# A Mamba-2 scan and an expert merge on one core: another opening, and the carried state turned by half for odd sequences only

## The chip, the cores and the metric

The kernel runs on one core of a Trainium2 chip. The metric is the device time of one execution in microseconds (us). The engines are TensorE (PE, its weight loads PEld), VectorE (DVE), ScalarE (ACT), GpSimd (POOL) and SyncE (SP), which issues nearly all transfers (DMA) here; SP's and ACT's issues appear in the profile as SPq and ACTq. A page of the profile shows one execution. All arithmetic is in 32-bit floats; each matmul appears in the trace as two records, one for each of its two passes.

## What is computed

```python
# x (4, 8, 768, 32), a (4, 8, 768), B and C (4, 8, 768, 16), chunk = 32
for c in range(nc):
    cum = np.cumsum(la, axis=-1)                       # la = log of clipped a
    L = np.exp(cum[:, :, :, None] - cum[:, :, None, :]) * causal
    M = np.einsum('bhin,bhjn->bhij', Cc, Bc) * L
    y_intra = np.einsum('bhij,bhjd->bhid', M, xc)
    y_inter = np.einsum('bhin,bhnd->bhid', Cc, state) * np.exp(cum)[:, :, :, None]
    y[:, :, sl] = y_intra + y_inter
    Bx = np.einsum('bhjn,bhjd->bhjnd', Bc, xc) * decay_from_j[:, :, :, None, None]
    state = decay_full[:, :, None, None] * state + np.sum(Bx, axis=2)
# bridge: tokens (3072, 256); 4 experts, w1 (256, 1024), w2 (1024, 256)
p = domain_probs / (domain_probs.sum(-1, keepdims=True) + 1e-09)
for e in range(E):
    out += p[:, e:e + 1] * (np.maximum(x @ w1[e], 0.0) @ w2[e])
```

The kernel needs the same values and cuts them in its own way.

## The kernel before

The four sequences of 768 positions are cut into 12 steps of 64 positions; a step covers all four sequences and all eight heads. The heads lie as four quarters `q` of 32 partitions with two heads `t` in each. For a step `k`:

- `score` (L488) multiplies B with C: 32 small matmuls in eight tiles of the array. `ctm` is C with one of each pair of heads masked out (`mask`, L484).
- The decay matrix LT comes from a scan over rows of `a` (`scan`, L599); `masked` (L503) multiplies scores by LT into MT, `fade` (L507) puts the decayed B beside it.
- `carried` (L516) multiplies the state S with the decayed C: 16 matmuls, each 32x32, four for each quarter, one per sequence `s`. `inner` (L524) adds MT times x into the same four banks `ys[s]`.
- `keep_inner` (L537) copies the outputs into yT; `keep_state` (L540) copies the new state into A, and `carry` (L844) transposes A and adds the old state times its decay.

The tokens of yT go through the two layers of the experts (`product`, L875), with sums of weights and of tokens formed so that fewer products are needed; `gated` (L911) applies max and the gate, `snap` (L886) and `seed` (L891) copy between banks and SBUF. The gates of an expert are a row of `p_d` in DRAM, spread over all partitions by a transfer (`load_gate`, L863); the first expert's are spread by matmuls instead (`spread_gate`, L646).

**Order.** The opening (L551 to L711) is written out by hand, in program order for each engine: loads, constants, `spread` of the decays (L656), the turn of the gates (L639), the scores, scans, inner products and copies of step 0. Everything behind it is put in order by `Plan` (L84): PE's order is the list `line`; for the rest, the plan plays the kernel through with estimated durations, and chooses order, buffers ("homes") and, where two engines can do a thing, the engine. It starts PE at `START` and the other engines at offsets to it (L1426). `fetch` (L754) asks for a pair of steps' transfers: `bc` (B and C), `ab` (decays, broadcast from `acut_d`), `ct` (C turned to where its state lies), `dec` (decays broadcast from `dec_d`), `xb` (x).

**The turn.** For sequence s the result of `carried` for quarter q goes to quarter (q + s) mod 4. So `ct` is loaded rotated (seven transfers, L439), `dec` is read from an offset of `dec_d`, and `keep_state` copies back in pieces: 1, 4, 2 and 4 copies for the four sequences.

```python
rows, to = slice(32 * q, 32 * q + 32), 32 * ((q + s) % NQ)      # carried
n = (P, P // NQ, P // 2, P // NQ)[s]                            # keep_state
```

Of the kernel before, what the change touches and what calls it, by code (L numbers as in the profile page):

```python
# [23 lines left out]
START = 11.0  # L24
# [59 lines left out]
class Plan:  # L84
# [12 lines left out]
    def add(self, on, fn, reads=(), writes=(), part=(), lag=None, due=None, reuse=None, two=False,  # L97
            port=True, after=None, kb=0, hold=0.0, pieces=1, lead=None):
# [13 lines left out]
        for v in part:  # L112
            w.needs.update(v.readers)
            v.writers = v.writers + [w]
        w.needs.discard(w)
# [233 lines left out]
def kernel(  # L349
# [89 lines left out]
    def load_turned(m, ct):  # L439
        for s in range(NSEQ):  # L440
            src = xbc[s * NC + m][:, OCT:]
            lo = P // NQ * s
            nc.sync.dma_start(out=ct[:P - lo, s], in_=src[lo:])  # L443
            if lo:
                nc.sync.dma_start(out=ct[P - lo:, s], in_=src[:lo])
# [8 lines left out]
    def load_faded(m, dec):  # L454
        for s in range(NSEQ):
            src = dec_d[s, m, NT * s:NT * s + NH]
# [59 lines left out]
    def carried(ys, S, cts, first):  # L516
        for q in range(NQ):
            for s in range(NSEQ):
                rows, to = slice(32 * q, 32 * q + 32), 32 * ((q + s) % NQ)
# [17 lines left out]
    def keep_inner(s, yt, y):  # L537
        nc.scalar.copy(out=yt[:, :, s * L:s * L + L], in_=view(y)[:, :, 0:L])

    def keep_state(s, A, y, engine="ACT"):  # L540
        copy = nc.scalar.copy if engine == "ACT" else nc.vector.tensor_copy
        n = (P, P // NQ, P // 2, P // NQ)[s]
        for here in range(0, P, n):
            there = (here + P // NQ * s) % P
# [8 lines left out]
    a_dec = homes["V"][-2][:NSEQ * NC * NQ, 0]  # L553
# [5 lines left out]
    a_rows = a.rearrange("(p j k) (q t) s -> k j q p t s", p=NP, j=2, q=NQ)[0]  # L559
    for j, e in ((0, nc.sync), (1, nc.scalar)):  # L560
        e.dma_start(
            out=aq.rearrange("(q r) p t s -> r q p t s", q=NQ)[j], in_=a_rows[j])
    nc.scalar.dma_start(out=pr, in_=probs)
# [4 lines left out]
    load_forms(0, bc)  # L568
    load_tokens(0, xb)
    nc.sync.dma_start(out=a_sb, in_=a.rearrange("c (q t) s -> (c q) (t s)", t=NT))  # L570
# [28 lines left out]
    def scan(LT, src, lo):  # L599
# [7 lines left out]

    pairs = const.tile([P, T // P, 2], FP32)
# [11 lines left out]
    nc.gpsimd.tensor_copy(  # L620
        a_cut.rearrange("r (h t s) -> r h t s", h=2, t=NT),
        a_sb.rearrange("r (t h s) -> r h t s", h=2, t=NT))
    nc.gpsimd.memset(a_cut.rearrange("r (x s) -> r x s", s=L)[:, :, 0:1], 0.0)
    for s in range(NSEQ):
        n = NC * NQ
        nc.sync.dma_start(  # L626
            out=acut_d.rearrange("j k q h p t s -> p j (k q) h (t s)")[s // 2, s % 2],
            in_=a_cut[n * s:n * s + n].rearrange("r (h x) -> r h x", h=2))
    for fb in range(4, 8, 2):
        load_w1(fb, homes["W"][fb])  # L630
# [62 lines left out]
    for q in (2, 3):  # L693
        scan_quarter(0, LT, four[q], q)
# [780 lines left out]
```

## Time and profile before

| | us |
|---|---|
| median of 3 runs (lowest, highest) | 636.07 (635.37, 637.23) |
| the profiled execution | 636.93 |
| its span, first to last instruction | 635.1 |
| PE busy (matmuls) | 613.7 |
| VectorE busy | 504.8 |
| ScalarE busy | 289.9 |
| POOL busy | 145.5 |
| mean granted TensorE clock | 0.991 |

The DMA moved 123.72 MB, 195 GB/s on the mean. In the chain of work that ended last, PE has 88% of the span, DMA 6% and SP's queue 3%. Busy time of PE counts a matmul from its start to its modelled end, so neighbours overlap, and a matmul at a lower clock counts longer. A wait is put down to the instruction that released it. The times of a line are those of one execution.

### The profile page before, as it was taken

Reading aid. Unit: us, or ns where it says so; the run is one execution under the profiler, and the core shown is the slowest. Engines: PE = TensorE matmul, PEld = TensorE weight load, DVE = VectorE, ACT = ScalarE, POOL = GpSimd, SP = SyncE. Lnnn points to the kernel's source line nnn. Section 1 sums busy time; section 2 is a strip of 40 time slices with the busy share of each in tenths; the row PEclk is TensorE's granted clock in tenths of the full one; section 3 lists DMA queues with packets and bytes.
Section 4 is the critical chain, followed back from the end, with each engine's and each line's share of the span. In section 5 each row is a group of like instructions: output and inputs, shape, how many; then the busy total and the mean of one; then the engine's idle time right before and its main releaser. Section 6 shows DMA issues by size and latency. Waiting matters only on the chain.

```text
span 635.1 us, 11792 instructions
## 1 busy us (share of the span) xinstructions
PE 613.7 (97%) x4185; PEld 526.2 (83%) x4185; DVE 504.8 (79%) x887; ACT 289.9 (46%) x646; POOL 145.5 (23%) x163
## 2 busy tenths in 40 slices
PE   5988999999999999999999999999999999999995
PEld 2766788888888888888888888888888888888884
DVE  5279989899578588877878987969797977968783
ACT  2454465353345344644444344655443344555440
POOL 4021236534054247234545400000000000000000
PEclk9989989999999999999999999999999999999998
DMA  4597989879389878749999928546232329633002
GB/s 120 169 290 254 292 278 328 263 240 289 102 258 293 258 249 256 224 120 303 299 306 304 316 42 270 157 149 190 65 93 66 83 50 326 214 116 108 0 1 50
DMA packets 116418, 123.72 MB, mean 195 GB/s; under 512 B 29592, under 2 KB 84232, under 8 KB 116360
## 3 DMA queue, kind: packets, MB, share of 16 engines
q1 hardware_dynamic: 115988, 122.87, 62.8%
q8 instruction: 33, 0.54, 0.4%
q14 instruction: 25, 0.20, 0.1%
q10 hardware_dynamic: 372, 0.11, 0.1%
HBM read 97.94 MB, written 24.99 MB: 194 GB/s over the span
## 4 chain that ended last, share of the span: by engine, by line
PE 88%; DMA 6%; SPq 3%; DVE 1%; issue 1%; ACT 0%; POOL 0%; DVEq 0%; POOLq 0%; ACTq 0%
PE bank L879 85%; DMA bc<-in_xbc_dram 1%; DMA ab<-acut_d 1%; PE bank L531 1%; DMA w<-in_w_dram 1%; PE bank L494 1%; DMA v<-in_a_dram 1%; PE bank L520 1%; SPq L626 0%; SPq L443 0%; DMA ct<-in_xbc_dram 0%; DMA dec_d<-v 0%; SPq L465 0%; SPq L433 0%; SPq L457 0%
## 5 line engine op out<-in xcount | busy, mean ns | idle before, releaser
L879 PE MATMUL bank<-v,w 128*128 128x256 f32 x1816 | 433.0, 383 | 1.2 <-ACT gate L652 0.7
L879 PEld LDWEIGHTS bank<-v,w 128*128 128x128 f32 x1816 | 345.9, 192 | 52.5 <-issue 1.8
L879 PE MATMUL bank<-Y,w 128*128 128x256 f32 x824 | 211.9, 381 | 4.2 <-ACT bank L893 4.2
L906 DVE TENSOR_TENSOR v<-v,v 128x512 f32<-128x512 f32 x270 | 193.1, 746 | 25.7 <-ACT v L888 22.0
L879 PEld LDWEIGHTS bank<-Y,w 128*128 128x128 f32 x824 | 156.7, 191 | 27.0 <-ACT bank L893 5.5
L914 DVE SCALAR_TENSOR_TENSOR v<-bank,gate 128x512 f32<-128x512 f32 x172 | 117.2, 685 | 54.1 <-PE bank L879 38.9
L893 ACT COPY bank<-v 128x512 f32<-128x512 f32 (+1 forms) x201 | 111.9, 573 | 54.2 <-DVE v L906 34.4
L970 POOL TENSOR_TENSOR w<-w,w 128x256 f32<-128x256 f32 x97 | 94.5, 998 | 73.5 <-PE bank L879 36.3
L888 ACT COPY v<-bank 128x512 f32<-128x512 f32 x112 | 65.6, 585 | 97.4 <-PE bank L879 96.8
L1156 ACT COPY v<-bank 128x512 f32<-128x512 f32 x106 | 62.0, 585 | 99.3 <-PE bank L879 98.0
L906 POOL TENSOR_TENSOR v<-v,v 128x512 f32<-128x512 f32 x10 | 13.7, 1372 | 266.6 <-DVE v L906 164.5
L906 DVE TENSOR_TENSOR v<-bank,v 128x512 f32<-128x512 f32 x40 | 27.5, 688 | 10.0 <-PE bank L879 9.5
L1208 DVE TENSOR_TENSOR v<-v,v 128x256 f32<-128x256 f32 x54 | 22.0, 442 | 6.8 <-ACT v L1156 6.7
L601 DVE TENSOR_TENSOR_SCAN LT<-ab,diag 128x512 f32<-128x512 f32 x20 | 27.1, 1366 | 0.0
L1159 ACT COPY v<-bank 128x256 f32<-128x256 f32 x23 | 8.6, 373 | 38.1 <-PE bank L879 38.1
L970 POOL TENSOR_TENSOR w<-w 128x256 f32<-128x256 f32 x10 | 10.7, 1069 | 49.0 <-DVE v L906 24.8
L1055 DVE TENSOR_TENSOR bank<-bank,v 128x512 f32<-128x512 f32 x24 | 16.6, 692 | 5.9 <-PE bank L879 5.9
L797 POOL TENSOR_TENSOR u<-ct,dec 128x256 f32<-128x256 f32 x11 | 10.5, 957 | 41.9 <-DMA dec<-dec_d 18.3
L545 ACT COPY A<-bank 32x32 f32<-32x32 f32 (+2 forms) x61 | 10.8, 177 | 12.2 <-PE bank L531 11.6
L970 DVE TENSOR_TENSOR w<-w,w 128x256 f32<-128x256 f32 x41 | 16.2, 433 | 0.0
L531 PE MATMUL bank<-MT,xb 64*32 64x80 f32 (+1 forms) x768 | 11.7, 245 | 3.4 <-POOL MT L509 3.4
L505 DVE TENSOR_TENSOR MT<-bank,LT 128x512 f32<-128x512 f32 (+1 forms) x26 | 14.5, 618 | 0.4 <-PE bank L494 0.3
(77 smaller groups left out, 213.5 us busy)
## 6 DMA issues: line engine op xcount, KB each, us to landing
w<-w_d SPq DMA_DIRECT2D x138, 256.0 KB
w<-in_w_dram SPq DMA_DIRECT2D x126, 256.0 KB
w_d<-w SPq DMA_DIRECT2D x82, 256.0 KB
w<-in_w_dram SPq DMA_DIRECT2D x42, 128.0 KB
ab<-acut_d SPq DMA_DIRECT2D x20, 256.0 KB
xb<-in_xbc_dram SPq DMA_DIRECT2D x24, 192.0 KB
gate<-p_d SPq DMA_DIRECT2D x10, 384.0 KB
bc<-in_xbc_dram SPq DMA_DIRECT2D x6, 512.0 KB
```

Of the source, the lines that this page charges most:

```text
L505: engine.tensor_mul(MT[:, q, h, ..., 0:L], g, LT[:, q, h])
L531: nc.tensor.matmul(out=view(ys[2 * p + j])[32 * q:32 * q + 32, t, 0:w], lhsT=xb[rows, p, h * D:h * D + D], rhs=MT[rows, q, k % 2, p, t, 0: ...
L601: nc.vector.tensor_tensor_scan(out=LT.rearrange("r q h p t s -> r (q h p t s)")[:, lo:lo + w], data0=src, data1=diag.rearrange("r h s -> r ...
L879: nc.tensor.matmul(out=o, lhsT=w[:, j], rhs=x if half is None else x[:, j], start=(start and j == 0), stop=(j == 1), skip_group_check=True)
L888: act(.5, lambda e: nc.scalar.copy(out=flat(v), in_=bank.t), reads=[bank], writes=[v])
L893: act(.54 if to - lo > FB else .32, lambda e: nc.scalar.copy(out=bank.t[:, lo:to], in_=flat(v)[:, lo:to]), reads=[v], writes=[bank])
L906: plan.add(engines, lambda e: (on(e).tensor_add if sign > 0 else on(e).tensor_sub)(flat(v), whole(x), whole(y)), reads=[x, y], writes=[v], ...
L914: dve(D512, lambda e: nc.vector.scalar_tensor_tensor(out=h.t, in0=whole(x).rearrange("p (j m) -> p j m", j=JJ), scalar=0.0, in1=g.t[:, 2 * ...
L970: plan.add({"POOL": .72} if due else B256, lambda e, r=r, x=x, y=y, sign=sign: (on(e).tensor_add if sign > 0 else on(e).tensor_sub)(view(r ...
L1055: dve(D512, lambda e: nc.vector.tensor_sub(b5.t, b5.t, flat(t)), reads=[t], writes=[b5])
L1156: act(.5, lambda e: nc.scalar.copy(out=flat(v), in_=bank.t), reads=[bank], writes=[v])
L1208: plan.add(engines, lambda e: (on(e).tensor_add if sign > 0 else on(e).tensor_sub)(o[1](), x[1](), y[1]()), reads=[v for v in vs if v is n ...
```

## The change

In the opening:

- The probabilities `pr` are loaded first on ScalarE's queue, before the second half of `a`; the raw decays `a_sb` go before the tokens on SP's.
- Another idle matmul of two column blocks follows the first two, and three filler matmuls of 256 columns stand before `inner`.
- `turn_gates` and both `spread` come before `mask`; the stores of `p_d` go from ScalarE's queue to SP's.
- `spread_gate` comes right behind, before `score`, into the upper halves of two banks whose lower halves the scores use; two copies take the place of one.
- One quarter instead of two goes by way of ScalarE and POOL (`aside`); three instead of two are masked on VectorE.
- `a_dec` is one scan of 256 columns with restarts, instead of four scans; `dec_d` is stored before the copies of yT and A, which alternate ScalarE and VectorE for yT, and are on ScalarE for A.
- The cut decays (`a_cut`, the four stores into `acut_d`) and the first `ct` leave the opening for the planned part; the loads of `ab` get the stores as explicit needs. The weights w1 of blocks 4 and 6 and w2 of blocks 0 and 2 are loaded before `score` is written out.

In every step: the quarter for sequence s is (q + 2s) mod 4, so even sequences are not turned and odd ones by half. `ct` is loaded by three transfers instead of seven, `keep_state` needs 1, 2, 1 and 2 copies.

The plan's start goes from 11 to 10, and the engines' offsets are others.

```diff
-START = 11.0
+START = 10.0
...
     def load_turned(m, ct):
-        for s in range(NSEQ):
-            src = xbc[s * NC + m][:, OCT:]
-            lo = P // NQ * s
-            nc.sync.dma_start(out=ct[:P - lo, s], in_=src[lo:])
-            if lo:
-                nc.sync.dma_start(out=ct[P - lo:, s], in_=src[:lo])
+        src = xbc.rearrange("(p j k) r w -> k j r p w", p=NP, j=2)[m]
+        dst = ct.rearrange("r (p j) x -> j r p x", j=2)
+        nc.sync.dma_start(out=dst[0], in_=src[0][..., OCT:])
+        for h in range(2):
+            nc.sync.dma_start(
+                out=dst[1][L * h:L * h + L], in_=src[1][L - L * h:P - L * h][..., OCT:])
...
-            src = dec_d[s, m, NT * s:NT * s + NH]
+            src = dec_d[s, m, NH // 2 * (s % 2):][:NH]
...
-                rows, to = slice(32 * q, 32 * q + 32), 32 * ((q + s) % NQ)
+                rows, to = slice(32 * q, 32 * q + 32), 32 * ((q + 2 * s) % NQ)
...
-        n = (P, P // NQ, P // 2, P // NQ)[s]
+        n = P // (1 + s % 2)
         for here in range(0, P, n):
-            there = (here + P // NQ * s) % P
+            there = (here + L * (s % 2)) % P
...
+    nc.scalar.dma_start(out=pr, in_=probs)
     for j, e in ((0, nc.sync), (1, nc.scalar)):
         e.dma_start(
             out=aq.rearrange("(q r) p t s -> r q p t s", q=NQ)[j], in_=a_rows[j])
-    nc.scalar.dma_start(out=pr, in_=probs)
...
     load_forms(0, bc)
+    nc.sync.dma_start(out=a_sb, in_=a.rearrange("c (q t) s -> (c q) (t s)", t=NT))
     load_tokens(0, xb)
-    nc.sync.dma_start(out=a_sb, in_=a.rearrange("c (q t) s -> (c q) (t s)", t=NT))
...
-            nc.scalar.dma_start(
+            nc.sync.dma_start(
                 out=p_d.rearrange("e k h s x -> h (e k) s x")[h], in_=p_sb[:, L * h:L * h + L])
 
-    def spread_gate(bank, gate):
-        g = bank.rearrange("r (s x) -> r s x", s=NSEQ)
+    def spread_gate(banks, gate):
         for s in range(NSEQ):
             nc.tensor.matmul(
-                out=g[:, s], lhsT=ident[:rows, s:s + 1].to_broadcast([rows, P]),
-                rhs=p_sb, start=(s == 0), stop=True, skip_group_check=True)
-        nc.scalar.copy(
-            out=gate[:, :4].rearrange("r (h y) (z x) -> r h (y z) x", h=2, z=2),
-            in_=g.rearrange("r s (h x) -> r h s x", h=2))
+                out=banks[s // 2][:, P * (2 + s % 2):][:, :P],
+                lhsT=ident[:rows, s:s + 1].to_broadcast([rows, P]),
+                rhs=p_sb, start=(s % 2 == 0), stop=True, skip_group_check=True)
+        for p in range(NP):
+            nc.scalar.copy(
+                out=gate[:, :4].rearrange("r (h y) (z x) -> r h (y z) x", h=2, z=2)[:, :, 2 * p:2 * p + 2],
+                in_=banks[p][:, 2 * P:].rearrange("r (s h x) -> r h s x", s=2, h=2))
...
     idle(BANK[6])
     idle(BANK[7], 3)
+    idle(BANK[6], 2)
     spread(0, four)
-    mask(0, ctm, bc)
     turn_gates(seven[3])
     spread(1, four)
+    mask(0, ctm, bc)
+    spread_gate(seven[1:3], homes["gate"][0])
+    for fb in range(4, 8, 2):
+        load_w1(fb, homes["W"][fb])
+    for fb in range(0, 4, 2):
+        load_w2(fb, homes["W"][fb + 1])
     score([0], ctm, bc, seven)
-    for q in range(2):
+    for q in range(NQ):
         scan_quarter(0, LT, four[q], q)
-        aside(q, seven[q])
-    for q in (2, 3):
-        scan_quarter(0, LT, four[q], q)
+        if q == 0:
+            aside(q, seven[q])
     fade(0, MT, xb, LT)
-    for q in (2, 3):
+    for _ in range(3):
+        nc.tensor.matmul(
+            out=seven[0][:, 2 * P:], lhsT=one.to_broadcast([P, P]),
+            rhs=one.to_broadcast([P, 2 * P]), start=True, stop=True, skip_group_check=True)
+    for q in (1, 2, 3):
         masked(nc.vector, [0], q, MT, parts(seven[q], 1), LT)
     inner(0, seven, xb, MT, L + N, True)
-    for s in range(NSEQ):
-        keep_inner(s, yT0, seven[s])
-    keep_state(0, A0, seven[0])
-    spread_gate(seven[0], homes["gate"][0])
-    for s in range(1, NSEQ):
-        keep_state(s, A0, seven[s])
-    for i in range(4):
-        nc.vector.tensor_tensor_scan(
-            out=a_dec[:, L * i:L * i + L], data0=a_sb[:, L * i:L * i + L],
-            data1=zeros[:NSEQ * NC * NQ, :L], initial=1.0, op0=ALU.mult, op1=ALU.add)
+    nc.vector.tensor_tensor_scan(
+        out=a_dec, data0=a_sb, data1=a_first, initial=0.0, op0=ALU.mult, op1=ALU.add)
     for z in range(2):
         nc.sync.dma_start(
             out=dec_d.rearrange("s k (z q t) x -> z (s k) q (t x)", z=2, t=NT)[z], in_=a_dec)
+    for s in range(NSEQ):
+        keep_inner(s, yT0, seven[s], (nc.scalar.copy, nc.vector.tensor_copy)[s % 2])
+    for s in range(NSEQ):
+        keep_state(s, A0, seven[s])
...
-    done = plan.run(line, now, {"PE": now, "DVE": now - .6, "ACT": now + 1.0, "POOL": now - 2.0,
-                                "SP": now + 1.0})
+    done = plan.run(line, now, {"PE": now, "DVE": now, "ACT": now + 1.0, "POOL": now - 1.5,
+                                "SP": now - 0.9})
```

## The prediction

> **What bounds the kernel now.** I read the page first (which engine is full, and in which slices), then the table of stretches, then TensorE's waits, then the timeline of the opening and of the one long stall behind it. The page:
>
> ```profile
> PE 613.7 (97%) x4185; PEld 526.2 (83%) x4185; DVE 504.8 (79%) x887; ACT 289.9 (46%) x646; POOL 145.5 (23%) x163
> ```
>
> TensorE is busy for 613.7 of 635.1 us: what is to be gained lies in its 21 idle us, and in time at a low clock, which counts as busy. The table of stretches (from:to, length, then busy time and instructions of PE, PEld, DVE, ACT, POOL, then granted clock, DMA share, GB/s) says where:
>
> ```profile
> 0.00:10.00 10.00, 6.93 (x53) 3.15 (x53) 2.80 (x16) 2.75 (x5) 4.13 (x15) 1.00 0.61 161
> 10.00:20.00 10.00, 5.22 (x91) 4.08 (x76) 6.32 (x13) 3.42 (x16) 2.75 (x6) 1.00 0.30 88
> 20.00:30.00 10.00, 9.64 (x65) 7.09 (x64) 3.31 (x8) 4.60 (x11) 0.84 (x1) 1.00 0.56 176
> 30.00:40.00 10.00, 7.56 (x117) 5.37 (x116) 4.79 (x12) 4.80 (x18) 0.64 (x1) 0.85 0.96 283
> 40.00:50.00 10.00, 9.78 (x43) 7.82 (x42) 9.32 (x25) 5.55 (x12) 3.53 (x2) 0.98 1.01 274
> ```
>
> Nearly 8 idle us lie before 20 us, 2.4 in 30 to 40, where the clock also falls to 0.85; from 40 on VectorE (9.3 of 10) and the DMA (1.01) are full. From 100 to 600 PE idles 0.15 us in 500, so the change can win nothing there, only lose. TensorE's waits, longest first:
>
> ```profile
> PE bank L879 <- ACT bank L893: 4.2, 4, 2.3
> PE bank L531 <- POOL MT L509: 3.4, 1, 3.4
> PE bank L520 <- DVE v L914: 2.4, 1, 2.4
> PE bank L640 <- POOL pc L614: 2.1, 1, 2.1
> ```
>
> The second and the fourth belong to the opening. Its timeline (start, length, engine, line):
>
> ```profile
> 5.87 0.26 POOL L609 TENSOR_TENSOR pairs<-pr 128x48 f32<-128x48 f32 x1 [3.51 <-DMA pr<-in_probs_dram]
> 9.55 1.62 ACTq L643 DMA_DIRECT2D p_d<-p_sb  x2
> 11.21 0.65 ACT L672 COPY w<-bank 128x256 f32<-128x256 f32 x2 [2.83 <-DMA p_d<-p_sb]
> 11.67 1.41 POOL L505 TENSOR_TENSOR MT<-w,LT 128x256 f32<-128x256 f32 x2 [1.05 <-ACT w L672]
> 13.03 0.65 POOL L509 TENSOR_TENSOR MT<-xb,LT 128x256 f32<-128x256 f32 x1
> 13.73 1.42 PE L531 MATMUL bank<-MT,xb 64*32 64x80 f32 x64 [3.39 <-POOL MT L509]
> 15.86 2.08 PE L649 MATMUL bank<-p_sb,ident 96*128 96x128 f32 x8 [0.71 <-ACT A L545]
> 17.98 0.58 ACT L652 COPY gate<-bank 128x512 f32<-128x512 f32 x1 [2.17 <-PE bank L649]
> 18.61 6.02 PE L879 MATMUL bank<-v,w 128*128 128x256 f32 x16 [0.68 <-ACT gate L652]
> ```
>
> Read it backwards: the first product (18.61) waits for the gate's copy, that for the gate's matmuls (2.08), those for the first state copy, that for the inner products (13.73), those for two masks and the fade on POOL, POOL for ScalarE's copies, and ScalarE had stood on the issue of the p_d stores (9.55 to 11.17). And the clock: the 16 records from 18.61 take 6.02 us, 16 later ones take 3.81 (below). Single records stand 0.427 us apart until 23.3 and 0.213 after it, so the products begin at half clock. The stall behind:
>
> ```profile
> 29.36 3.81 PE L879 MATMUL bank<-v,w 128*128 128x256 f32 x16 [0.36 <-DMA w<-in_w_dram]
> 33.10 0.41 PE L520 MATMUL bank<-cts,S 32*32 32x128 f32 x6
> 35.21 1.29 DVE L914 SCALAR_TENSOR_TENSOR v<-bank,gate 128x512 f32<-128x512 f32 x2 [6.76 <-DMA gate<-p_d]
> 35.95 0.49 PE L520 MATMUL bank<-cts,S 32*32 32x128 f32 x26 [2.44 <-DVE v L914]
> ```
>
> The carried products stop after 6 of 32 records, because a bank is held by a gating that waits for a gate transfer issued at 28.88. The record of the clock shows half rate for 3.41 us right after it (36.98 to 40.39); the stall of 2.5 us at 78.0 is followed by the same.
>
> **Part 1, the opening up to the first product.** The probabilities go out first on ScalarE's queue, ahead of the bulk: a small transfer issued at 1.22 had landed by 3.60, so pr is there about 3.3 instead of 5.87; the chain L609 to L614 took 1.7 us (5.87 to 7.58), which puts pc at about 5.1. The idle matmuls grow by two column blocks, 0.85 us at the cold rate, and end at 4.8 instead of 3.94; that delays spread(0) from 4.33 to 4.8, and covers what the second half of a loses behind pr (0.36). spread(0) ends at 6.05, the turn of the gates at 6.5 (0.45), p_sb's copy at 6.85 (0.26). From there a cold and a warm column, as matmuls run at 0.427 or 0.213 per 256 columns. spread(1): 7.1 warm, 7.75 cold. spread_gate (1.04 or 2.08): 8.2, 9.8. Its two copies (a 128x256 copy on ScalarE is 0.37; ahead of them the masks, 0.91 after bc's landing at 6.99): 9.0, 10.6. score has to wait for them, as they read the same banks (before, the scan of the first half of a bank waited for the matmul into its second half, 2.13 us): 0.69 in the row at 24.57, 1.16 in the one at 9.18, so 9.7, 11.75. ScalarE's one remaining copy: 10.0, 12.1; POOL's mask 0.70 and fade 0.65: 11.4, 13.45. VectorE takes three masks instead of two (0.37 each) and is done before POOL. The three filler matmuls (6 records) come after ScalarE's copy: 11.3, 14.65. inner (0.9 or 1.42): 12.3, 16.1. Two of the four yT copies go to VectorE, and the first bank comes free after 0.38 and 0.23 on ScalarE and some 0.2 of passing on: **13.2 warm, 16.9 cold, against 18.61**. Which one? PE would be busy without a gap from 0.77 to beyond 8; before, its longest unbroken run ended at 4.0. The clock changes in the record at steps of 3.41 us, and the full stretch 19.91 to 23.33 was followed by the full rate, while 16.50 to 19.91, 80% full, was not. Any run of 6.8 us holds one full step, so I take warm: **-5.4** (bounds -1.7 and -5.5). The single a_dec scan (one 256-wide scan, 0.61, for four of 0.43) lies beside the inner products on VectorE: 0; uncovered it would be 0.6.
>
> **Part 2, the cold products.** 18.61 to 23.33 at half rate is 2.36 us lost: **-2.4** (bounds 0 and -2.4).
>
> **Part 3, SP's queue and the gate stall.** p_d's two stores now stand on SP and wait for p_sb (6.85); behind them are w4, w6 and two w2 blocks (0.97 + 0.97 issue), which before went out at 13.99 and 19.97, so this costs nothing. Then dec_d waits for the scan: out at about 11.5 to 13.2 instead of 21.0 to 22.7. Into the planned part go the four acut_d stores (3.31) and the turned form, three transfers for seven (about 1.5 for 3.5). From dec_d to the gate's issue there are, in before's order, dec 2.56, two weights 0.97, xb 1.36; with ct 1.5 that gives 19.6, or 22.9 if the planner puts acut_d ahead, though ab needs it much later. So the gate goes out 9.3 (or 6.0) earlier and PE needs it 7.8 earlier: the 2.7 us stall shrinks by 1.5, and as a gap of 1.57 at 54.8 left the clock alone, the half-rate stretch (1.7) goes too: **-3.2** (bounds +1.8 and -4.4). Late next is VectorE.
>
> **Part 4, what comes back.** PE reaches the stretch 40 to 84 about 11 us earlier. Up to 80 us the DMA had moved 18.1 MB (the GB/s column); at 290 GB/s, the best rate of the table, they take 62.4, and PE would want them by 69. That just fits, at a use that the kernel never holds (0.81 in 100 to 200), and VectorE has to do the 46 us it does from 20 to 80 in that time. I give back a third: **+3.5** (bounds 0 and +11).
>
> **Part 5, the carried products.** Now sixteen products use sixteen tiles of the array (352 records, 11 calls, 0.43 us each). After it sequences 0 and 2 share one, as do 1 and 3: eight tiles, twice each. In the trace's single records sixteen first passes start 6.7 ns apart from 97.077, their second passes from 97.210; in score a tile takes its next record every 109 ns. If only the tile waits, each call grows by two records, 0.22 us, eleven calls: +2.4. If a product that waits for its tile stops all behind it, each of the four quarters costs a tile's two records more: 4 x 0.22 = 0.84 with what overlaps, +9.2. I take **+2.4**, since second passes already start after later first passes, so order is not kept strictly; neither end is excluded.
>
> [...]
>
> **Part 6, small.** State copies fall from 11 to 6 per step (121 to 66, 0.18 each); ScalarE and VectorE hide them except near 396, where seven on VectorE end in a gap of 0.53 at PE: **-0.3**. The decay rows, the buffers held later and the planner's start times cost nothing by themselves, but all orders except PE's are planned anew, and a mistake like the one at 78 costs 2.5 + 1.7.
>
> Sum: -5.4 - 2.4 - 3.2 + 3.5 + 2.4 - 0.3 = -5.4. The profiled execution took 636.93 (span 635.1 and 1.8 around it), 0.86 above the median of 636.07. That gives 631.5 on its scale, **630.7 on the median's**.
>
> **Rivals.** (1) Blocked order in the carried products, ending slower: L520 instead of the opening; 9.2 for 2.4 makes the sum +1.4, 637.5, and past the 0.3% mark (1.9 us, about what a measurement of this kernel can tell from no change) once the opening gives half a us less than I took. For it: waits stop everything behind them (6 of 32 records). Against it: the passes. (2) The whole gain comes back in 40 to 84 (11 instead of 3.5): +2.1, about 638, or 636 if some stays. For it: VectorE at 9.3 to 9.9 of 10. Against it: VectorE idles 12 of 20 us before. (3) Nothing comes back, and the stall at 78 isn't planned again: -8.9, and up to -4 more, 623 to 627. (4) The opening stays cold: parts 1 and 2 give 1.7 for 7.8, but less comes back (about a third of 5, 1.6): -1.2, 635. It counts with (2).
>
> **How the numbers follow.** Forecast 0.50 (own range 626.5 to 634.2), (1) 0.22, (2) with (4) 0.15, (3) 0.13. Faster: 0.49 + 0.13 + 0.02 of (2); same: 0.07 of (1), 0.07 of (2), 0.01; slower: 0.15 of (1), 0.06 of (2). The range 623.5 to 639.5 leaves a tenth out on either side: the best of (3), and (1) with a poor opening.
>
> **What would show it.** First product near 13 and the records 0.213 apart from there; p_d on SP's queue and no wait of ScalarE for it; no half-rate stretch near 30; the wait for L914 near 1 us; L520's chain pieces 0.65 instead of 0.43 (near 1.3 would be rival 1); L545 at 66 copies. I am wrong if the first product comes after 16, or if PE's idle time after 20 us grows by over 4.

## The result, and the profile after

The changed kernel takes **633.14 us** (median of 6 runs, 631.51 to 634.51) against 636.22 of the kernel before (6 runs beside them, 635.37 to 637.79): a ratio of 0.9946, interval [0.9925, 0.9968], which is 3.4 us (2.0 to 4.8) faster. The profiled execution took 633.88 (span 632.1), 3.05 less than the one before. The forecast was 630.7, a gain of 5.4.

Lines in this trace are one to six higher than before: the product is L885 (L879), the gating L920 (L914), the seed L899 (L893), the carried products L521 (L520), the inner ones L532 (L531), the score L495 (L494), the mask L487 (L486). The page:

```profile
PE 613.7 (97%) x4193; PEld 527.0 (83%) x4193; DVE 504.3 (80%) x881; ACT 280.1 (44%) x597; POOL 137.3 (22%) x162
```

TensorE's busy time has not moved by a tenth of a us. So the page alone would say that TensorE lost 3 us of idle time and nothing else; the stretches (columns as before) say where, and that a good part of the gain has gone again:

```profile
0.00:10.00 10.00, 7.95 (x64) 4.64 (x65) 5.01 (x20) 3.65 (x8) 4.88 (x19) 1.00 0.69 181
10.00:20.00 10.00, 8.87 (x127) 6.61 (x127) 6.83 (x16) 3.89 (x13) 2.11 (x4) 1.00 0.73 228
20.00:30.00 10.00, 9.54 (x130) 7.43 (x130) 4.69 (x11) 5.40 (x17) 1.39 (x2) 1.00 0.83 271
30.00:40.00 10.00, 9.09 (x40) 6.90 (x38) 9.85 (x26) 5.96 (x12) 0.00 (x0) 1.00 0.81 273
60.00:80.00 20.00, 14.47 (x143) 11.81 (x142) 12.49 (x31) 8.74 (x24) 3.49 (x5) 0.83 1.02 300
```

Up to 40 us TensorE is now busy for 35.5 us instead of 29.4, with no half-rate stretch behind 4.2. Then 60 to 80: 14.47 of 20 instead of the 18.17 it had before, at a mean clock of 0.83. The clock's record shows half rate for 6.83 us there (72.48 to 79.3), and full rate from then to 628.9. (Times of the clock's record, here and below, count from a point 0.05 us ahead of the rows' zero.) The opening:

```profile
5.55 0.26 ACT L632 COPY p_sb<-bank 96x128 f32<-96x128 f32 x1 [1.58 <-PE bank L631]
5.84 1.67 SPq L634 DMA_DIRECT2D p_d<-p_sb  x2
6.09 1.16 PE L639 MATMUL bank<-p_sb,ident 96*128 96x128 f32 x8
8.06 1.21 PE L495 MATMUL bank<-ctm,bc 32*64 32x128 f32 x32 [0.81 <-ACT ctm L487]
11.58 1.05 PE L532 MATMUL bank<-MT,xb 64*32 64x80 f32 x64 [0.27 <-POOL MT L510]
13.11 1.10 PE L885 MATMUL bank<-v,w 128*128 128x256 f32 x4 [0.48 <-ACT A L546]
```

The first product starts at 13.11 (18.61 before), and its four records take 1.10 us, the full rate. And the new stall:

```profile
63.90 0.37 SPq L437 DMA_DIRECT2D bc<-in_xbc_dram  x1
66.36 0.71 PE L521 MATMUL bank<-cts,S 32*32 32x128 f32 x32
71.21 1.70 ACT L487 ACTIVATE ctm<-bc,tmask 128x256 f32<-128x256 f32 x4 [6.09 <-DMA bc<-in_xbc_dram]
72.82 0.57 ACT L899 COPY bank<-v 128x512 f32<-128x512 f32 x1
73.45 2.08 PE L885 MATMUL bank<-Y,w 128*128 128x256 f32 x4 [5.53 <-ACT bank L899]
```

Read it backwards. The products at 73.45 wait for a seed, a 0.57 us copy into their bank. The seed follows the instruction before it without a wait of its own: it stands on ScalarE behind four instructions of `mask`, and ScalarE stands idle for 6.09 us until the `bc` that they mask has landed, 7.3 us after its issue at 63.90. The scores that need these masks start at 120.86. So work that had nearly 50 us to spare stopped work that had none.

To see how the lead over the kernel before grows and shrinks, I took the start of the same records in the traces (TensorE's order is one list, the same in all); this table is called the ladder below. Its last column is the first experiment. Its times, too, count from 0.05 us ahead of the rows' zero, and each column is one execution.

| record | before | after | difference | masks held: difference |
|---|---|---|---|---|
| first product | 18.66 | 13.16 | -5.50 | -5.44 |
| first score behind it | 24.62 | 17.43 | -7.19 | -7.13 |
| carried, call 1 | 33.15 | 25.32 | -7.83 | -7.19 |
| second score | 63.45 | 52.91 | -10.54 | -9.84 |
| carried, call 2 | 76.87 | 66.41 | -10.46 | -9.76 |
| carried, call 3 | 97.08 | 91.22 | -5.85 | -12.98 |
| third score | 125.31 | 120.91 | -4.40 | -12.77 |
| carried, call 11 | 422.84 | 419.64 | -3.21 | -11.03 |
| last matmul | 628.62 | 625.62 | -3.00 | -10.83 |

At 66 us the changed kernel is 10.5 ahead; at 121 it is 4.4 ahead.

### The profile page after: what moved, and what is told of

It is laid out like the page before. It is cut to its first block, busy times and chain, and to the rows that moved or that the text cites. A ratio compares the mean times of both kernels' runs of the same rounds, so it can differ in the third digit from the quotient of the medians.

```text
span 632.1 us, 11732 instructions
## 1 busy us (share of the span) xinstructions
PE 613.7 (97%) x4193; PEld 527.0 (83%) x4193; DVE 504.3 (80%) x881; ACT 280.1 (44%) x597; POOL 137.3 (22%) x162
## 4 chain that ended last, share of the span: by engine, by line
PE 87%; DMA 5%; DVE 4%; SPq 2%; ACT 1%; issue 1%; POOL 0%; ACTq 0%; DVEq 0%; POOLq 0%
PE bank L885 83%; DMA bc<-in_xbc_dram 2%; PE bank L532 1%; DVE w L976 1%; DMA w<-in_w_dram 1%; DMA w_d<-w 1%; PE bank L495 1%; PE bank L521 1%; DVE v L920 1%; DMA gate<-p_d 1%; DVE v L912 0%; DVE LT L602 0%; SPq L458 0%; ACT ctm L487 0%; ACT bank L899 0%
## 5 line engine op out<-in xcount | busy, mean ns | idle before, releaser
L885 PE MATMUL bank<-v,w 128*128 128x256 f32 x1816 | 429.7, 381 | 1.9 <-DVE v L920 1.0
L885 PEld LDWEIGHTS bank<-v,w 128*128 128x128 f32 x1816 | 343.8, 190 | 52.0 <-issue 2.4
L885 PE MATMUL bank<-Y,w 128*128 128x256 f32 x824 | 213.1, 382 | 7.3 <-ACT bank L899 7.1
L912 DVE TENSOR_TENSOR v<-v,v 128x512 f32<-128x512 f32 x271 | 197.8, 760 | 27.7 <-ACT v L894 22.4
L885 PEld LDWEIGHTS bank<-Y,w 128*128 128x128 f32 x824 | 157.0, 191 | 31.3 <-ACT bank L899 9.0
L920 DVE SCALAR_TENSOR_TENSOR v<-bank,gate 128x512 f32<-128x512 f32 x172 | 117.2, 685 | 45.3 <-PE bank L885 32.9
L899 ACT COPY bank<-v 128x512 f32<-128x512 f32 (+1 forms) x201 | 111.6, 573 | 46.4 <-DVE v L912 31.4
L976 POOL TENSOR_TENSOR w<-w,w 128x256 f32<-128x256 f32 x96 | 89.0, 948 | 76.0 <-PE bank L885 45.9
L912 POOL TENSOR_TENSOR v<-v,v 128x512 f32<-128x512 f32 x9 | 12.4, 1383 | 254.6 <-DVE v L912 152.3
L539 ACT COPY v<-bank 128x128 f32<-128x128 f32 x46 | 10.4, 270 | 21.5 <-PE bank L532 17.7
L976 DVE TENSOR_TENSOR w<-w,w 128x256 f32<-128x256 f32 x42 | 18.5, 476 | 0.0
L546 DVE COPY A<-bank 64x32 f32<-64x32 f32 (+1 forms) x52 | 9.2, 188 | 8.0 <-ACT v L539 6.1
```

Source lines behind the costliest of these rows:

```text
L885: nc.tensor.matmul(out=o, lhsT=w[:, j], rhs=x if half is None else x[:, j], start=(start and j == 0), stop=(j == 1), skip_group_check=True)
L899: act(.54 if to - lo > FB else .32, lambda e: nc.scalar.copy(out=bank.t[:, lo:to], in_=flat(v)[:, lo:to]), reads=[v], writes=[bank])
L912: plan.add(engines, lambda e: (on(e).tensor_add if sign > 0 else on(e).tensor_sub)(flat(v), whole(x), whole(y)), reads=[x, y], writes=[v], ...
L920: dve(D512, lambda e: nc.vector.scalar_tensor_tensor(out=h.t, in0=whole(x).rearrange("p (j m) -> p j m", j=JJ), scalar=0.0, in1=g.t[:, 2 * ...
L976: plan.add({"POOL": .72} if due else B256, lambda e, r=r, x=x, y=y, sign=sign: (on(e).tensor_add if sign > 0 else on(e).tensor_sub)(view(r ...
```

## The experiments

Except in TensorE's list, each kernel's order is planned anew, so a small edit moves much else; "masks held" below is the changed kernel with the edit of the first experiment, and most later kernels are built on it. They ran in three groups, each with its own runs of the kernel before: mask_late_after, mask_late_before, turn_only and turn_undone (its median 637.25); m_quarter, m_no_turn, m_gate_back and m_no_fill (635.87); m_pe_late, m_old_transfers, m_pd_act and m_no_turn_seq (636.37). Between groups, ratios compare better than medians, and I give both where it matters.

### Where the gain went: the masks held back

Theory A: the loss of 6 us between 66 and 121 is the masks' place in ScalarE's queue. The rival, the prediction's second: VectorE and the DMA are full there, and would take the gain in another way. The edit lets the plan start a mask at most 12 us before it is due:

```diff
-            act(.76, lambda e, k=k: mask(k, b["ctm"].t, b["bc"].t), reads=[b["bc"]], part=[b["ctm"]])
+            act(.76, lambda e, k=k: mask(k, b["ctm"].t, b["bc"].t), reads=[b["bc"]], part=[b["ctm"]], lead=12.0)
```

> The changed kernel, with one edit to the plan: the masks of C on ScalarE (L487) may start no sooner than 12 us before the plan's latest time for them, so that they no longer stand ahead of a seed (L899) while bc is still under way. Theory A (the 5.5 us wait of TensorE at 67.7 to 73.5, and the 6.8 us at half clock behind it, come from ScalarE's queue standing on a mask that waits for bc): the wait goes and so does the half clock, 5.5 + 3.4 = 8.9 us, less what comes next in that stretch (VectorE is at 9 of 10 there), some 2 us: 633.1 - 7 = 626. Rival (VectorE and the DMA are full from 40 on, whatever ScalarE does): the same time is lost in other waits, L885 on VectorE or on loads, and the total stays within 1.5 us of 633.1.

Measured: **625.75** (625.27 to 626.28), ratio 0.9815 [0.9799, 0.9832]. The place, and the stretch (columns as before):

```profile
67.06 0.71 PE L521 MATMUL bank<-cts,S 32*32 32x128 f32 x32
67.53 0.59 ACT L899 COPY bank<-v 128x512 f32<-128x512 f32 x1 [1.71 <-DVE v L920]
68.55 1.13 PE L885 MATMUL bank<-Y,w 128*128 128x256 f32 x4
```

```profile
60.00:80.00 20.00, 19.64 (x180) 16.58 (x179) 19.64 (x42) 11.04 (x29) 7.67 (x8) 1.00 1.01 302
```

The seed runs as soon as its source is there, and TensorE is busy for 19.64 of 20 us at the full clock, with VectorE at 19.64 of 20 and the DMA at 1.01. That is as full as the rival said, and it costs nothing: no lead is lost between 66 and 121 us. It grows by 3, since the old stall at 78 is gone too, and then falls by 0.2 per carried call. Theory A holds, the rival falls. This version beats both kernels, the one before by 1.85% and, by the quotient of the two ratios, the changed one by 1.3%.

The same line changed in the kernel before, whose stall at 78 has the same cause:

> The kernel before, with the same edit to the plan (masks of C no sooner than 12 us before their latest time). Theory A: its wait of 2.3 us at 78.0 to 80.5 and the 3.4 us at half clock behind it go: 2.3 + 1.7 = 4.0 us, less 1 for what comes next: 636.2 - 3 = 633. Rival (VectorE and the DMA give it back): within 1 us of 636.2.

Measured: 635.74 (634.37 to 639.04), ratio 0.9974 [0.9957, 0.9991]: 1.7 us (0.6 to 2.7) where theory A gave 3. In its trace the stall and its half-rate stretch are gone, -3.9 between the second and third call of the carried products; but 0.6 us is lost ahead of it and 0.7 behind. The repair works where it is put, and is worth 1.7 there in all; the change alone is worth 3.4; both together are worth 11.8. What the opening wins is kept only where no mask stands in front of it.

### The turn

Alone, in the kernel before (these two edits, and with them `load_turned`, the offset of `dec`, and the numbers of loads and copies that the plan counts with):

```diff
-                rows, to = slice(32 * q, 32 * q + 32), 32 * ((q + s) % NQ)
+                rows, to = slice(32 * q, 32 * q + 32), 32 * ((q + 2 * s) % NQ)
...
-        n = (P, P // NQ, P // 2, P // NQ)[s]
+        n = P // (1 + s % 2)
```

> The kernel before, with the turn by half for odd sequences alone (three loads of ct for seven, six state copies for eleven) and the old opening. Theory (a tile of the array used twice costs two more records of 0.109 us, and nothing behind it is held): each of the 11 calls of the carried products 0.636 for 0.431, +2.26 us; fewer copies give back 0.5 at most near 396: 636.2 + 2 = 638, if the stalls around 33 and 78 stay as they are. Rival (fewer copies and transfers are worth more than the tiles cost, as ScalarE and SP's queue are behind in the first 85 us): TensorE's waits before 85 us fall by over 2 us and the total is 636 or less.

Measured: 638.18 (636.05 to 641.61), ratio 1.0028 [1.0008, 1.0049], +1.8 us. A call of the carried products, counted from its first record to the first record of the inner products behind it (a row's length is 0.07 longer), takes 0.636 us instead of 0.431, so TensorE pays 11 x 0.205 = 2.26. That is shown. That the total also fits is in part luck: the plan moved other things, the old stall at 78 is gone here, and a half-rate stretch of 6.83 us stands at 35.96 to 42.79 where before had 3.41. The twelve runs spread over 5.6 us, and the profiled one (636.15) is among the fastest: its last matmul comes 1.1 us earlier than in the kernel before. So the +1.8 of the medians is not the price of the tiles alone.

The same lines taken back in the changed kernel:

> The changed kernel with the old turn by quarters (seven loads of ct, eleven state copies) and the new opening. Theory: 11 calls at 0.431 for 0.636, -2.26 us, and +0.5 of copies: 633.1 - 1.8 = 631.3, if the stalls of the stretch 25 to 120 stay. Rival (the fewer copies and transfers carry part of the gain): waits of TensorE in 25 to 120 grow by over 2 us, and the total is 633 or more.

Measured: 633.30 (631.44 to 636.95), ratio 0.9939 [0.9918, 0.9961], no different from the changed kernel; the rival's total came, the theory's 631.3 did not. Calls are back at 0.431, so 2.3 us of TensorE are won, but ahead of the second call new waits cost more than that: 1.45 instead of 0.38 at 14.5, and 1.76 instead of 0.46 at the first carried call, which waits for the gate, with a half-rate stretch of 3.41 us from 28.7. The stall behind the masks is there as before (4.51 at 70.3). The profiled execution ends 1.7 earlier than that of the changed kernel, which the medians do not confirm. This says nothing of the turn by itself, so the masks were held:

> The changed kernel with the masks held back (625.8 us so far) and, beside it, the old turn by quarters: seven loads of ct, eleven state copies, sixteen tiles of the array. With the long stall out of the way the price of the turn should stand alone. Theory (a tile used twice costs two records, 0.205 us a call): 11 x 0.205 = 2.3 us less for the calls, and +0.5 for copies near 390: 625.8 - 1.8 = 624. Rival (the fewer copies and transfers of the half turn are worth as much): 625.8 or more, with new waits of TensorE of 2 us before 120.

Measured: 631.26 (628.82 to 633.71), ratio 0.9922 [0.9895, 0.9950]: slower than masks held with the half turn, by 5.5 us of the medians (6.8 by the ratios), against my theory; the rival is what came. In the trace the eleven state copies on ScalarE (2.10 us for 1.18) are followed by a wait of 1.44 us at 16.1 where masks held has 0.38; the seven loads of `ct` hold SP for 4.4 us (12.33 to 16.75) where three take 2.6, the gates go out 1.3 to 1.4 later (21.76 and 22.86), and the bank is held:

```profile
27.78 1.29 DVE L920 SCALAR_TENSOR_TENSOR v<-bank,gate 128x512 f32<-128x512 f32 x2 [6.43 <-DMA gate<-p_d]
28.53 0.49 PE L521 MATMUL bank<-cts,S 32*32 32x128 f32 x26 [1.86 <-DVE v L920]
```

Half rate follows (28.97 to 32.38), and a further wait of 1.99 stands at 96.9, where ScalarE waits for `u` ahead of a copy. The ladder is 4.7 behind masks held at the third score, and comes back by 0.2 per call to 2.8 at the end; this execution (628.82) is the fastest of the six, so about half of the 5.5 is in no trace. So the half turn's price on TensorE is real, and in this opening the half turn as a whole wins more than that back. How much of the 5.5 is queue, how much is copies and how much the luck of a plan stays open: the edit changes all three.

With no turn at all, four products of a call share one tile. The edit: `to = 32 * q`, `ct` in one transfer, one copy of the state per sequence.

> The changed kernel with the masks held back and no turn at all: all four sequences of a quarter use one tile of the array, four tiles... used four times each for the carried products; one load of ct, four state copies. Theory (only the tile's own records count, 0.109 us each): a call goes from 0.636 to 0.636 + 4 x 0.109 = 1.07 us, 11 calls +4.8 us: 625.8 + 4.8 = 630.6, less up to 1 for fewer copies and loads. Rival (a product that waits for its tile holds all behind it): the four quarters run one after another, a call 4 x 8 x 0.109 = 3.5 us, +31 us.

Measured: 644.59 (644.04 to 645.20), ratio 1.0134 [1.0113, 1.0155]. Neither size was right: a call takes 2.385 us, between 1.07 and 3.5, and 11 x 1.75 = 19.2 us more for the calls fit the 18.8 between the medians. The single records say why: a quarter's records start at 0, 0.133, 0.242, 0.351 and 0.460, and the first of the next quarter at 0.466, when the waiting quarter has come to its third product (each product is two records). By these times and the program's order, everything behind stood while two products waited for the same tile; once only the last one waited, the next quarter started. To see whether it is the order or the tile's own work, the same kernel with the loops changed:

```diff
-        for q in range(NQ):
-            for s in range(NSEQ):
+        for s in range(NSEQ):
+            for q in range(NQ):
```

> The kernel without any turn (644.6 us, 2.385 us a call of the carried products), with one edit: the loop over sequences outside the loop over quarters, so that a tile of the array comes again after four products instead of at once; the plan is the same. Theory (it is not the use of a tile that costs, but that products which wait for their tile hold those behind them): the four tiles run side by side, a call is 0.13 + 7 x 0.109 + 0.2 = 1.1 us, 11 calls 14 us less, 630.5. Rival (the tile's own load and stream are slower in this form, whatever the order): a call stays above 2 us and the total above 642.

Measured: 632.02 (630.05 to 634.00), ratio 0.9937 [0.9918, 0.9956], 12.6 us less than the other order. One call in the one and in the other:

```profile
87.60 2.46 PE L517 MATMUL bank<-cts,S 32*32 32x128 f32 x32
```

```profile
87.09 1.07 PE L517 MATMUL bank<-cts,S 32*32 32x128 f32 x32
```

It was the order: with three products between two that share a tile the call takes 1.005 us (its row's length less 0.07), not far above the 0.87 of a tile's own eight records at 0.109. The half turn's 0.636 is still less.

### What in the opening is worth the time

Five kernels on masks held. First, the gates spread late again, behind the first state copy and into one whole bank, in the old order of the opening:

```diff
-    spread_gate(seven[1:3], homes["gate"][0])
...
-    for s in range(NSEQ):
+    keep_state(0, A0, seven[0])
+    spread_gate(seven[0], homes["gate"][0])
+    for s in range(1, NSEQ):
         keep_state(s, A0, seven[s])
```

> The changed kernel with the masks held back, and the spreading of the first gates put back behind the first state copy, into a whole bank, with one copy; all else in the opening stays new, and the plan is the same. Theory (the gate's matmuls and copy stood on the path to the first product): first product 1.0 for the matmuls at full clock, 0.6 for the copy and 0.3 for two handovers later, 13.2 + 1.9 = 15.1, and the total 625.8 + 1.9 = 627.7. Rival (the first product is held by yT and its bank all the same, or the time comes back in the stretch at 25 to 50 where TensorE waits for VectorE): first product 15.1, total within 0.7 of 625.8.

Measured: 624.82 (624.01 to 630.19), ratio 0.9841 [0.9806, 0.9876], no different from masks held; the first product comes at 13.41, not 15.1.

```profile
7.20 0.70 PE L495 MATMUL bank<-ctm,bc 32*64 32x128 f32 x32 [0.99 <-ACT ctm L487]
11.58 1.16 PE L640 MATMUL bank<-p_sb,ident 96*128 96x128 f32 x8 [0.47 <-ACT A L546]
13.41 1.99 PE L885 MATMUL bank<-v,w 128*128 128x256 f32 x8 [0.68 <-ACT gate L643]
```

The 1.16 us of gates are back in front of the first product, but the score is 0.70 long instead of 1.21 and starts 0.9 earlier than in the changed kernel. There it stands behind the gates on TensorE and shares two banks with them; which of the two makes it longer was not tried. The early spread wins on one side what it loses on the other.

Then the early fillers left out, the idle matmuls and the three products of ones ahead of `inner`:

```diff
-    idle(BANK[6], 2)
...
-    for _ in range(3):
-        nc.tensor.matmul(
-            out=seven[0][:, 2 * P:], lhsT=one.to_broadcast([P, P]),
-            rhs=one.to_broadcast([P, 2 * P]), start=True, stop=True, skip_group_check=True)
```

> The changed kernel with the masks held back, without the third idle matmul and without the three filler matmuls ahead of the inner products; the plan is the same. Theory (unbroken work at the start brings the full clock early and keeps it): TensorE is idle from 9 to 11.6, and the products begin in a half-rate step of 3.4 us, or reach the full rate one step later: 1.7 to 2.4 us more, 625.8 + 2 = 628. Rival (the early gates and spreads alone keep the clock): the records stand 0.213 apart from the first product on, first product up to 0.1 earlier as nothing stands ahead of the inner products, total within 0.5 of 625.8.

Measured: 626.09 (623.92 to 627.53), ratio 0.9837 [0.9808, 0.9866]: no change that shows. The half-rate stretch did come, 11.57 to 14.99, which is 1.7 us of lost work; but the first product came at 12.93, and at the first carried call the kernel was 0.4 ahead of masks held. Masks held waits there, 0.52 us for `cts` and 0.51 for the gating; this kernel has neither wait, and at the second score it is 0.9 ahead.

That raised the question whether an early first product is worth anything. Theory T: what counts is when the transfers go out (the gates, `dec`, weights); an early product only runs into the next wait. Theory P: what is won at the first product is won at the end. Nine useless matmuls delay the products and nothing else:

```diff
+    for _ in range(9):
+        nc.tensor.matmul(
+            out=seven[0][:, 2 * P:], lhsT=one.to_broadcast([P, P]),
+            rhs=one.to_broadcast([P, 2 * P]), start=True, stop=True, skip_group_check=True)
```

> The changed kernel with the masks held back (625.8 us so far), and nine useless matmuls of 256 columns on TensorE between the state copies and the first product: 9 x 0.43 = 3.9 us of TensorE in the place where the new opening had won 5.5; the transfers, the plan and all else stay. Theory T (the gain is carried by the transfers: TensorE waits for gates, decays and VectorE between 25 and 50 anyway): first product at 17.1, but only 0 to 1.5 us left of it at the score of 53.6, total 626 to 627.5. Rival P (the gain is TensorE's earlier start): the 3.9 us stay in full, total 629.7.

Measured: 626.98 (626.21 to 627.52), ratio 0.9853 [0.9836, 0.9871].

```profile
12.79 4.19 PE L710 MATMUL bank<-const-float32-1.0 128*128 128x256 f32 x18 [0.41 <-ACT A L546]
16.82 3.69 PE L889 MATMUL bank<-v,w 128*128 128x256 f32 x16
28.33 0.71 PE L521 MATMUL bank<-cts,S 32*32 32x128 f32 x32
```

The first product is 3.65 us later than in masks held, the first carried call 2.4, the second score 0.8 and the end 0.9. The call at 28.33 runs in one piece: the waits that masks held has up to here (0.38 at 15.1, 0.52 and 0.51 at the call) are gone, and with them part of the delay. From the first product to the second score TensorE waits 1.9 us in all, where masks held waits 3.5. By medians the end moves by 1.2, by ratios by 2.4 (0.9 to 4.0, so the ratios alone do not exclude 3.9); in the traces a quarter of the delay is kept. That speaks against P; T's numbers came.

The other half of T, the old order of all transfers in the new opening (`acut_d` and `ct` early on SP, `p_d` on ScalarE, weights behind):

> The changed kernel with the masks held back, and the old transfers: the four stores of the cut decays and the first ct back in the opening, two pairs of weights at their old places around them, the stores of p_d on ScalarE's queue; the rest of the new opening stays (the first pr, early gates, idle and filler matmuls, one scan, fewer copies). Theory T (transfers carry the gain): SP's queue is 3 to 4 us later at dec and at the gates; the carried products of step 1 wait until about 30 instead of 27, and 3 to 4 us are left at the end: 629. If ScalarE also stands on p_d's issue, the first product comes 1 to 2 us later as well. Rival P: first product as before 13.2 or 1 later, total 626 to 627.

Measured: 634.54 (632.53 to 637.24), ratio 0.9970 [0.9952, 0.9988]. That is 8.8 us of medians, more than either theory said, and most of the gain over the kernel before. The size is nearly three times what T gave. But this run does not part the theories: its first product comes at 19.19, 6.0 us later than in masks held, and the second score 7.4, the end 6.4 later. So the transfers delayed TensorE's start as well. One piece of it stood out in the trace, so it was tried alone: the two `p_d` stores on ScalarE's queue.

```diff
-            nc.sync.dma_start(
+            nc.scalar.dma_start(
                 out=p_d.rearrange("e k h s x -> h (e k) s x")[h], in_=p_sb[:, L * h:L * h + L])
```

> The changed kernel with the masks held back, and the two stores of p_d on ScalarE's queue again, nothing else; the plan is the same. Theory (the stores' issue, some 1.6 us, stands ahead of the masks of C and the copies on ScalarE): masks about 1.6 later, first product 1 to 1.6 later, at 14.2 to 14.8; as transfers carry the gain, the total stays within 1 of 625.8. Rival (TensorE's start carries it): total 626.8 to 627.4.

Measured: 629.33 (627.90 to 629.75), ratio 0.9887 [0.9867, 0.9907]: 3.6 us of medians (4.6 by the ratios), where I had expected within 1.

```profile
5.67 0.26 ACT L632 COPY p_sb<-bank 96x128 f32<-96x128 f32 x1 [1.69 <-PE bank L631]
8.94 1.61 ACTq L634 DMA_DIRECT2D p_d<-p_sb  x2
10.66 0.91 ACT L487 ACTIVATE ctm<-bc,tmask 128x256 f32<-128x256 f32 x2 [4.73 <-DMA p_d<-p_sb]
11.62 1.67 PE L495 MATMUL bank<-ctm,bc 32*64 32x128 f32 x32 [4.26 <-ACT ctm L487]
```

`p_sb` is there at 5.93, but the issue goes out only at 8.94 and takes 1.6, so ScalarE's masks come at 10.66, the score at 11.62 and the first product at 18.46, with half rate from 11.27 to 18.1. What the issue itself waited for between 5.93 and 8.94 no row names, and it was not tried.

The first product is 5.3 us later than in masks held, the second score 3.65, the end 3.65. The decays are late as well (`dec_d` is stored at 15.14 instead of 11.19, and `dec` and the gates follow it on SP), but TensorE does not wait for them. Its longest waits:

```profile
PE bank L495 <- ACT ctm L487: 4.3, 1, 4.3
PE bank L885 <- ACT bank L899: 1.9, 4, 0.7
```

No row of that list, which goes down to 0.2 us, names a transfer, the gating or `cts`, and from the first product to the second score the waits are 2.1 us. So here the late start itself is what stays, and T alone does not hold. Both runs fit one account, that TensorE makes up a delay only as far as it had waits to give, 3.5 us of them in masks held: 2.8 of 3.65 us were made up with the useless matmuls, 1.6 of 5.3 here. Why less here is not shown. The old transfers without these stores cost more in another way: that kernel is 0.7 us behind this one at the first product and 3.8 at the second score. Which of those transfers does it was not tried.

## Why the prediction was right or wrong

**The sign and the main mechanism were right; the gain came out 2 us smaller.** In the terms of its sum, on the profiled executions ("cold" is at half rate):

| part | predicted | measured | from |
|---|---|---|---|
| 1, first product | -5.4 | -5.5 | ladder |
| 2, cold products | -2.4 | -2.3 | ladder, to carried call 1 |
| 3, SP's queue and the gate | -3.2 | -2.9 | to the second score, less 0.2 for call 1 |
| 4, what comes back | +3.5 | +5.7 | 6.06 from call 2 to the third score, less 0.4 for two calls |
| 5, carried products | +2.4 | +2.3 | 11 x 0.205 |
| 6, small | -0.3 | -0.2 | behind 121: +1.4, less 8 x 0.205 |
| sum | -5.4 | -2.9 (spans: -3.0) | |

**The step that failed is Part 4**, in its reason as well as in its size. It gave back a third of the lead because VectorE and the DMA are full in 40 to 84. They are, and with the masks held they stay so (VectorE 42.6 of these 44 us, the DMA 1.00) while the whole lead is kept. What came back was mainly one wait: 5.53 us behind the call at 66 where before had 2.29 at 78 (+3.2), and behind it 6.83 us at half rate for 3.41 (+1.7). A wait of 1.01 at 116.2, for VectorE, came on top, and the rest of the stretch gave 0.3 back. The prediction had seen the thing: Part 6 says that a mistake like the one at 78 costs 2.5 + 1.7. But it was read as a possible accident and priced at nothing. Before's trace had shown the mechanism, a mask after 3.45 us of idle ScalarE, the seed behind it, the product behind that:

```profile
79.02 0.91 ACT L486 ACTIVATE ctm<-bc,tmask 128x256 f32<-128x256 f32 x2 [3.45 <-DMA bc<-in_xbc_dram]
79.84 0.58 ACT L893 COPY bank<-v 128x512 f32<-128x512 f32 x1
80.47 1.29 PE L879 MATMUL bank<-Y,w 128*128 128x256 f32 x4 [2.29 <-ACT bank L893]
```

The change brings TensorE to that place 10 us earlier, but `bc` went out only 6.1 us earlier (63.90 for 70.03), through a DMA as full as before (a busy share of 1.02 in 60 to 80, before 1.01), and all four instructions of `mask` now stood ahead of the seed, where before had two. The question to ask was what stands in ScalarE's queue ahead of the seed, and when its transfer will land.

**Part 1 came out right, in part by luck.** Its -5.4 followed one chain (gates early, score, inner products) at the full clock, and its end came out to the tenth: 13.2, measured 13.11. The steps on the way did not: `p_sb`'s copy ended at 5.81 and not 6.85, while POOL's fade took 1.07 us and not 0.65, and the inner products ended at 12.63 and not 12.3. And m_gate_back shows the early gates to be worth nothing that the total shows, m_no_fill the same for the fillers, and m_pe_late that of 3.65 us at the first product 0.8 are left at the second score. The pieces of the opening that did show in the total are the stores of `p_d` off ScalarE (3.6 us of medians) and all transfers in the new order (8.8, these stores included). Part 1 had the p_d issue in its reading of the old chain, but gave it no price of its own.

**Part 3** gave the gate's issue as 19.6 with the stall left at 1.2. It was 20.58, and the stall 0.46 (2.44 before, in the same row):

```profile
20.58 0.46 SPq L872 DMA_DIRECT2D gate<-p_d  x1
25.27 0.62 PE L521 MATMUL bank<-cts,S 32*32 32x128 f32 x6
26.35 0.69 PE L521 MATMUL bank<-cts,S 32*32 32x128 f32 x26 [0.46 <-DVE v L920]
```

So the issue gained 8.3 us and not 9.3, only 0.5 more than TensorE. The stall shrank by 2.0 all the same, because the gating followed the issue after 5.0 us (at 25.60), where before it took 6.3 (28.88 to 35.21); the prediction had not counted on that. The half-rate stretch near 30 went, as said, and the copies of L546 are 66.

**Part 5** took the value at which only the tile waits, and that is what the calls show. In single records (the call at 91.17) eight first passes start in pairs within 0.09 us, and then each tile takes its next record every 0.109. Had each product that waits for its tile stopped all behind it, a call would have taken 0.43 + 0.84 = 1.27 us by the prediction's estimate; it took 0.636, and first passes of later quarters started ahead of products that waited for their tile: eight passes that start within 0.09 us lie on eight tiles, as a tile takes a record every 0.109 us. But the order was not free either: with one tile four times in a row a call took 2.385, and 1.005 with the same products in another order.

**The rivals.** Rival 1 (blocked order) fell for the half turn; with no turn at all it came true in part (2.385 us a call). Rival 2 had the right stretch, but a wrong cause and nearly twice the size (11 us back for 5.7). Rival 3 (nothing comes back, 623 to 627) is what masks held measured, 625.75: it is the change without the mistake. Rival 4 fell: the first products are at the full clock. That one step of half rate in the opening changes nothing that the total shows (m_no_fill) neither the forecast nor rival 4 had.

## What to carry to other kernels

ScalarE took its queue in order here (the seed at 72.82 stood behind masks that had waited 6.09 us): for every wait on a transfer in the trace, ask what stands behind it on that engine and who needs that, above all where a change moves the place earlier and the transfer cannot follow; work with tens of us to spare must not be queued ahead of work with none. Move DMA issues off an engine that computes on the critical path (here the two `p_d` stores off ScalarE, 3.6 us of medians). And before an early start is counted as a gain, delay it by useless work and add up the waits behind it: as far as the bottleneck waits there anyway, an earlier start wins nothing, and beyond that it does (in m_pe_late 2.8 us of a delay of 3.65 were made up, with 3.5 us of waits to give).

## What the runs showed of the hardware

- Read from the times of the records and the program's order: one product that waited at a tile of the array did not hold those behind it, two that waited at the same tile did. In a call of the half turn (0.636 us; the changed kernel at 91.17), six tiles had one waiting product each while others still started, eight first passes within 0.09 us; the call cost 0.2 us over one without shared tiles (0.431). Four in a row on one tile (m_no_turn, 2.385 us, a quarter every 0.466) cost 1.95 us over it, four with three others between each two (m_no_turn_seq, 1.005) 0.57.
- The clock went to half in whole steps of 3.41 us: one step after waits of TensorE of 1.86 (m_quarter), 2.44 and 2.29 us (the kernel before), two after 4.26 (m_pd_act), 4.51 (turn_undone) and 5.53 us (the changed kernel). But no length of a wait decides it alone: half rate followed 1.58 us at 33.5 in mask_late_before and 1.89 at 24.2 in m_no_turn, and did not follow 1.85 at 47.7 in mask_late_before, 1.86 at 24.3 in m_no_turn_seq and 1.99 at 96.9 in m_quarter. What decides stays open.
- The issue of two small stores stopped a computing engine: in m_pd_act it went out at 8.94 and took 1.61 us, and ScalarE did nothing between 5.93 and 10.66, where in the changed kernel it began its masks at 7.11.
